# Where the scales of twelve weight blocks come from: column sums on TensorE, or squares on ScalarE and a sum over partitions on GpSimd

## The chip, the cores and the metric

One core of a Trainium2 chip runs the whole kernel. The metric is the device time of one execution in microseconds. The profile is of one such execution on the same core; its times are microseconds from the start of the span, unless they are marked ns.

Names of the engines in the profile: PE is TensorE (PEld its weight loads), DVE is VectorE, ACT is ScalarE, POOL is GpSimd, SP is the engine that issues most of the DMAs. A "q" behind a name means its sequencer, mostly DMA issues.

## The reference

Causal attention with a learned decay as bias, then a gated feed-forward network over all tokens. Sizes: 8 batches, 8 heads, 576 positions, head size 64, so 4608 tokens of width 512; hidden width 1536.

```python
scores = q @ k.T / sqrt(64);  cum = cumsum(max(s, 0))
scores = where(causal, -1e9, scores + min(-(cum_i - cum_j), 0))
attn   = softmax(scores) @ v                      # per head
x      = attn, heads side by side                 # 4608 x 512
gate   = sigmoid(x @ w_gate);  val = x @ w_val    # 512 x 1536 each
out    = (gate * val) @ w_out                     # 1536 x 512, float32
```

`q`, `k`, `v` and `s` come as float32. The three weights come as 64-bit floats, which the kernel reads as pairs of 32-bit integers.

## The kernel before, in words

**Matrix products.** Operands are split into a high and a low part in f16 and multiplied in three products (high x high, high x low, low x high). So that the parts fit f16, every operand is first multiplied by a power of two, its scale. The scale divides out again behind the product. The change is about how the scales of the weights are found.

**Weights: eighteen steps.** `wsteps` lists them. Steps 0 to 11 are for the gate and value weights, step f for the f-th block of 128 hidden columns (both matrices: 4 x 2 x 128 = 1024 numbers a partition). Steps 12 to 17 are for the output weights, two blocks of 128 hidden rows each. One step (`weight_step`) does:
- `load_weight`: DMAs of the 64-bit numbers into a room, issued from ACT's queue for steps 2 and later. Rooms are few. Before step n, `weight_step` issues loads whose room an earlier step has left.
- `decode_weight`: 64-bit floats into 32-bit ones, by one ACT copy (L298) and three DVE passes over 128x1024 (L299, L300, L301). L299 writes a first rough form `m`, whose upper 16 bits serve as a bf16 number for the column sums; L301 gives the final `a`.
- `column_bound`: eight TensorE matmuls of `ones` with that bf16 form (L310) add the columns up over all partitions into a PSUM bank. A DVE maximum over the 128 sums with its accumulator output (L313) makes one number of it. The PSUM bank is the one tag "av" (one buffer, otherwise the attention output's) in the first 40 ticks, and the tag "o" (two buffers, otherwise the output rows') after that.
- Two small DVE instructions (L332, L334) make the power of two from it.
- `split_weight`: an ACT copy with that scale gives the high part (L337), a DVE pass the low part (L338).

`column_bound` needs `m` alone, so it may run beside L300 and L301. The function `split_weight` has a second way, taken where `decode_weight` gives no `m`; before, that is for weights that come as float32, so never here. It squares `a` on ACT with a sum along each partition, adds the 128 sums over partitions on POOL (`partition_all_reduce`, result in every partition), and makes the power of two from that with `pow2_of` (two small DVE instructions).

**The order of the work.** The body is one loop over 332 ticks, five a head (one for each tile of query rows), 64 heads. The first eight heads (ticks 0 to 39) run in float32 on PE (functions named `n_...`); later ones in split f16: scores (`s_part`, L489 and L491), bias and maximum on DVE (L529), exponent on ACT (L530), high and low part of the probabilities (`p_part`: ACT L534, DVE L539 and L547), a transposing DMA, output (`av_part`, L562 to L567), `x_part` and `split_x`. Weight steps 0 to 5 are spread over ticks up to 32. From tick 44 (`NE`) on, the first two groups of 256 tokens go through the first feed-forward product, 24 units in eight ticks; each unit is 24 matmuls (L714, into the tag "gv" of two banks), a tanh on ACT (L719) and one DVE instruction (L721). Ahead of every third unit stand three weight steps and the scales of three blocks for the tanh (`inverse_weights`, `ffn_scale`); the steps of the output weights stand between the later units. After the last unit `hidden_scale` needs all scales, and only then come the output products of these two groups (`ffn_mid`: L729, L730; `ffn_out`: L744). `late_slots` then closes the pool `lp` (`ones`, the first room, small rest) and takes its place for more buffers of `x`.

The loop gives program order and priorities, not the order on the engines. `first()` raises attention of ticks 44 to 86 above the rest, so weight steps and units are work in the background there. The order on each engine is laid out when the program is built, from priority and from the time at which each instruction is expected to be ready. On the chip each engine then takes its own queue strictly in that order.

**POOL's queue** holds the all-reduces for the scales of q and k (L406) and of v (L196), the broadcasts of the decay rows (L451), masks (L511, from head 16 on), memsets (L459, L471) and the DMAs of the output rows.

The lines that the chip's time hangs on most in the units:

```python
with first(NE <= n < NOFF):
    s_part(i, NTL - 1 - t)
...
if f < NF and f % WLA == 0:
    while wnext["step"] < f + WLA:
        weight_step()
    inverse_weights(0, slice(f, f + WLA))
    ffn_scale(0, slice(f, f + WLA))
while f == 8 and wnext["step"] < NF + 1:
    weight_step()
while f >= NF and wnext["step"] < min(f + NF + WLA, len(wsteps)):
    weight_step()
emit_unit()
```

Of the kernel before, what the change touches and what calls it, by code (L numbers as in the profile page):

```python
# [10 lines left out]
F32 = mybir.dt.float32  # L11
# [7 lines left out]
P = 128  # L19
# [6 lines left out]
def tile_attention_then_gated_ffn(  # L26
# [23 lines left out]
    NTL = len(TILES)  # L50
# [4 lines left out]
    NN = H  # L55
# [7 lines left out]
    pp = ctx.enter_context(tc.tile_pool(name="pp", bufs=2, space=bass.MemoryType.PSUM))  # L63
# [160 lines left out]

    wide = w_gate.dtype == I64
    wst, wdec, wtot = {}, {}, {}

    rows_out = cp.tile([P, 2 * DM], F32, name="io")
    t2big = cp.tile([P, 2 * NF * GT], F32, name="t2f")
# [23 lines left out]
    def room(n):  # L253

        o, f = wsteps[n]
        if o == 0:
            return raw[f % 3], dec[f % 3], n - 3
        i, j, last = outroom[f // 2]
        return raw[i], dec[j], last
# [30 lines left out]
    def decode_weight(n):  # L290

        o, f = wsteps[n]
        r, a, _ = room(n)
        if not wide:
            return a.bitcast(F32), None
        m = w2all[:, f // 2].rearrange("p l h x n -> p (l h x n)") if o else w1[f].rearrange("p c g l n -> p (c g l n)")
        m = m.bitcast(I32)
        nc.scalar.activation(a.bitcast(F32), r[:, :, 1].bitcast(F32), AF.Copy, scale=2.0 ** -112)  # L298
        nc.vector.tensor_scalar(m, a, 3, 0x7FFFFFF8, ALU.logical_shift_left, ALU.bitwise_and)  # L299
        nc.vector.scalar_tensor_tensor(a, a, -0x80000000, m, ALU.bitwise_and, ALU.bitwise_or)  # L300
        nc.vector.scalar_tensor_tensor(a, r[:, :, 0], 29, a, ALU.logical_shift_right, ALU.bitwise_or)  # L301
        return a.bitcast(F32), m

    def column_bound(n, m):

        top = m.bitcast(BF16).rearrange("p (n t) -> p n t", t=2)[:, :, 1]
        early = wnext["tick"] < NTL * NN
        ps = pp.tile([P, 512], F32, tag="av" if early else "o", name=f"wps{n}", **({"bufs": 1} if early else {}))
        for c in range(8):
            nc.tensor.matmul(ps[:, :P], ones, top[:, c * P : (c + 1) * P], start=c == 0, stop=c == 7)  # L310
        tot = wp.tile([P, 1], F32, tag="wst", name=f"wtot{n}")
        junk = lp.tile([P, P], BF16, tag="wj", name=f"wj{n}")
        nc.vector.tensor_scalar(junk, ps[:, :P], 2.0 ** -100, None, ALU.max, ALU.max, accum_out=tot)  # L313
        return tot

    def split_weight(n, a, m):

        o, f = wsteps[n]
        if o:
            hi, lo = (w2all[:, f // 2, l].rearrange("p h x n -> p (h x n)") for l in range(2))  # L320
        else:
            a = a.rearrange("p (c n) -> p c n", n=P)
            hi, lo = (w1[f].rearrange("p c g l n -> p (c g) l n")[:, :, l] for l in range(2))
        if m is None:
            ss = wp.tile([P, 1], F32, tag="wss", name=f"wss{n}")
            nc.scalar.activation(hi, a, AF.Square, accum_out=ss)
            tot = wp.tile([P, 1], F32, tag="wst", name=f"wtot{n}")
            nc.gpsimd.partition_all_reduce(tot, ss, P, ADD_REDUCE)
            pow2_of(wscale[:, o, f : f + 1 + o], tot, f"w{n}")
        else:  # L330
            e = wp.tile([P, 1], I32, tag="xe", name=f"xe_w{n}")
            nc.vector.tensor_scalar(e, column_bound(n, m).bitcast(I32), 0x7F800000, None, ALU.bitwise_and)  # L332
            dst = wscale[:, o, f : f + 1 + o]
            nc.vector.tensor_scalar(dst.bitcast(I32), e.to_broadcast([P, 2]) if o else e, -1.0, 268.0 * 2.0 ** 23,  # L334
                                    ALU.mult, ALU.add)
        sc = wscale[:, o, f : f + 1]
        nc.scalar.activation(hi, a, AF.Copy, scale=sc)  # L337
        nc.vector.scalar_tensor_tensor(lo, a, sc, hi, ALU.mult, ALU.subtract)  # L338
# [21 lines left out]
        osc[b] = wp.tile([P, 1], F32, tag="osc", name=f"osc{b}", bufs=3)  # L360
        nc.vector.tensor_scalar(osc[b], gmax, sv[b][1], 2.0 ** 14, ALU.mult, ALU.mult)

    wnext = {"load": 0, "step": 0, "tick": 0}

    def weight_step():
        n = wnext["step"]
        while n and wnext["load"] < len(wsteps) and room(wnext["load"])[2] < n:
            if not NF <= wnext["load"] < NF + 2:
                load_weight(wnext["load"])
            wnext["load"] += 1  # L370
        split_weight(n, *decode_weight(n))
        wnext["step"] = n + 1
# [426 lines left out]
    for n in range(nticks + 12):  # L799
        if n == NTL * EARLY:  # L800
            more_room()
        i, t = divmod(n, NTL)
        wnext["tick"] = n
        if i < NN:
            with first():
                n_s(i, NTL - 1 - t)
# [7 lines left out]
        if 2 <= n < nticks + 2:  # L814
            a, z = divmod(n - 2, NTL)
# [5 lines left out]
        if 1 <= n < nticks + 1:  # L821
            a, z = divmod(n - 1, NTL)
# [7 lines left out]
        if 3 <= n < 3 + NTL * NN:  # L830
            with first():
                a, z = divmod(n - 3, NTL)
# [113 lines left out]
        if n >= NE and state["u"] < 2 * NF:  # L946
            fdone = min(NF, int((n - NE + 1) * FPT))
            while state["u"] < 2 * fdone:
                f = state["u"]
# [17 lines left out]
        m = n - (11 if n > 2 * NTL * H + 30 else 7)  # L967
# [42 lines left out]
```

## Time and profile before

| | |
|---|---|
| median of 3 runs | 1151.53 us (1150.67 to 1153.77) |
| the profiled execution | 1150.28 us, of it span 1148.5 us |
| PE busy | 1096.8 us (96%), 11868 matmuls |
| DVE busy | 756.4 us (66%) |
| ACT busy | 733.5 us (64%) |
| POOL busy | 199.9 us (17%) |
| mean granted clock of TensorE | 0.993 |

Busy times are shares of the whole span; the stages differ. A slice view cuts the span in 40 equal parts and gives the busy share of each in tenths. A view of windows gives busy time and, in brackets, the number of instructions for each engine in a stretch, then the granted TensorE clock. A list of waits gives who stood idle for whom, the total, how often, and the longest. A timeline gives start, length, engine, line, operation and what it writes from what; in square brackets stands the idle time ahead of it and what ended that. A chain is followed back from the last instruction to whatever released each step.

### The profile page before, as it was taken

The numbers are of one execution on the slowest core, as the hardware profiler recorded it, in microseconds if no ns is written. First come the engines' busy times: TensorE is split into PE (matmuls) and PEld (weight loads), VectorE is DVE, ScalarE is ACT, GpSimd is POOL, SyncE is SP. The second block draws the span as 40 slices with busy tenths as digits, with TensorE's granted clock in tenths as the row PEclk, the third lists the DMA queues.
The fourth block names the chain that finished last, engine by engine and source line by source line (L and its number), as shares of the span: only waits on it lengthen the run. The fifth ranks groups of instructions, "written<-read, shape, count | busy, mean of one in ns | idle before, by whom it ended". The sixth has DMA issues, their size and how long they took to land.

```text
span 1148.5 us, 30266 instructions
## 1 busy us (share of the span) xinstructions
PE 1096.8 (96%) x11868; PEld 861.6 (75%) x11868; DVE 756.4 (66%) x2212; ACT 733.5 (64%) x1437; POOL 199.9 (17%) x473
## 2 busy tenths in 40 slices
PE   6998878999999999999999999999999999999998
PEld 4776757757777887788777777778877787787775
DVE  6868989876787777665565667777777775222222
ACT  5869667867776777676665667778676765233222
POOL 3301101022232222121211122212221211000000
PEclk9999999999999999999999999999999999999999
DMA  9766986997989688866645488878787774000000
GB/s 282 218 189 140 181 178 144 174 200 154 178 159 187 150 186 158 154 139 135 148 87 130 90 175 163 170 144 175 152 159 146 142 123 88 13 20 20 1 19 19
DMA packets 445517, 157.63 MB, mean 137 GB/s; under 512 B 403583, under 2 KB 435839, under 8 KB 445374
## 3 DMA queue, kind: packets, MB, share of 16 engines
q1 hardware_dynamic: 418686, 127.38, 56.7%
q10 hardware_dynamic: 23328, 17.04, 4.9%
q0 software_dynamic: 3360, 11.27, 2.8%
q8 instruction: 93, 1.52, 0.6%
q14 instruction: 50, 0.41, 0.1%
HBM read 56.92 MB, written 9.58 MB: 58 GB/s over the span
## 4 chain that ended last, share of the span: by engine, by line
PE 72%; DMA 10%; DVE 6%; issue 5%; ACT 3%; SPq 3%; POOL 1%; ACTq 0%; DVEq 0%; POOLq 0%
PE gv L714 39%; PE o L744 21%; DMA v<-in_v_dram 3%; PE s L491 3%; PE s L489 2%; DMA T<-qk 2%; PE na_ps L662 1%; SPq L463 1%; DVE e L529 1%; PE av L564 1%; PE av L562 1%; PE av L563 1%; DMA qk<-in_q_dram 1%; DMA w2all<-in_moe_w_out_dram 1%; PE s L631 1%
## 5 line engine op out<-in xcount | busy, mean ns | idle before, releaser
L714 PE MATMUL gv<-x,w 128*128 128x256 f16 (+3 forms) x6912 | 619.2, 247 | 10.1 <-DVE t2f L721 9.1
L714 PEld LDWEIGHTS <-w 128*128 128x128 f16 x6912 | 536.0, 98 | 75.0 <-issue 11.5
L744 PE MATMUL o<-w2all,h 128*128 128x512 f16 x1296 | 313.7, 379 | 1.8 <-ACT h L729 1.8
L530 ACT ACTIVATE e<-e,em 128x576 f32<-128x576 f32 x280 | 153.2, 556 | 92.5 <-DVE em L529 89.8
L744 PEld LDWEIGHTS <-h 128*128 128x128 f16 x1296 | 123.3, 98 | 109.1 <-ACT h L729 2.1
L719 ACT ACTIVATE th<-gv,scb 128x256 f32<-128x256 f32 (+3 forms) x288 | 110.8, 410 | 138.6 <-PE gv L714 130.5
L721 DVE SCALAR_TENSOR_TENSOR t<-th,gv 128x256 f32<-128x256 f32 x192 | 80.0, 417 | 147.9 <-ACT th L719 146.8
L511 POOL TENSOR_SCALAR_AFFINE_SELECT rl<-rl 128x128 f32<-128x128 f32 (+1 forms) x240 | 85.8, 358 | 503.1 <-DVE em L529 462.3
L529 DVE CUSTOM_DVE_ANT_0 e<-s,rl,qkcf 128x576 f32<-128x576 f32 x280 | 151.5, 545 | 31.7 <-PE s L491 15.6
L729 ACT ACTIVATE h<-t,hsc 128x256 f16<-128x256 f32 x192 | 96.7, 504 | 92.4 <-DVE t L721 92.4
L539 DVE SCALAR_TENSOR_TENSOR p<-e,p 128x384 f16<-128x384 f32 x224 | 103.1, 500 | 45.1 <-ACT p L534 44.3
L730 DVE SCALAR_TENSOR_TENSOR h<-t,hsc,h 128x256 f16<-128x256 f32 x192 | 93.7, 488 | 44.9 <-ACT h L729 42.6
L534 ACT ACTIVATE p<-e 128x1152 f16<-128x1152 f32 x112 | 111.9, 1000 | 2.7
L489 PE MATMUL s<-T 128*128 128x288 f16 (+2 forms) x246 | 64.1, 278 | 7.8 <-DVE em L529 4.0
L562 PE MATMUL av<-v,pt 128*128 128x65 f16 x560 | 67.7, 193 | 2.2 <-DMA pt<-p 2.2
L451 POOL PARTITION_BROADCAST cr<-cr x63 | 59.4, 947 | 56.0 <-DMA cr<-cum_d 42.0
L563 PE MATMUL av<-v,pt 128*128 128x64 f16 x560 | 67.7, 192 | 0.0
L564 PE MATMUL av<-v,pt 128*128 128x65 f16 x560 | 67.6, 194 | 0.0
L491 PE MATMUL s<-T 128*128 128x288 f16 (+2 forms) x246 | 61.5, 277 | 4.0 <-DMA T<-T 3.9
L562 PEld LDWEIGHTS <-pt 128*128 128x128 f16 x560 | 52.5, 97 | 7.9 <-DMA pt<-p 3.1
L563 PEld LDWEIGHTS <-pt 128*128 128x128 f16 x560 | 52.5, 97 | 4.5
L564 PEld LDWEIGHTS <-pt 128*128 128x128 f16 x560 | 52.7, 97 | 0.2
(164 smaller groups left out, 1297.0 us busy)
## 6 DMA issues: line engine op xcount, KB each, us to landing
v<-v SPq DMA_DIRECT2D x56, 162.5 KB
out_dram<-io POOLq DMA_DIRECT2D x34, 256.0 KB, 3.2
v<-in_v_dram SPq DMA_DIRECT2D x64, 128.0 KB
T<-T SPq DMA_DIRECT2D x82, 72.0 KB
t2f<-in_v_dram SPq DMA_DIRECT2D x20, 288.0 KB
qk<-in_q_dram SPq DMA_DIRECT2D x17, 288.0 KB
qk<-in_k_dram SPq DMA_DIRECT2D x17, 288.0 KB
w2all<-in_moe_w_gate_dram ACTq DMA_DIRECT2D x7, 512.0 KB
```

Of the source, the lines that this page charges most:

```text
L491: nc.tensor.matmul(ps[:, : b_ - a], lhs, T[i][:, 2, a:b_], start=False, stop=not mask)
L529: nc.vector.tensor_tensor_reduce(e, ps, r, c, MASKED, ALU.add, ALU.min, acc)
L530: nc.scalar.activation(e_t[t][:, :w], e_t[t][:, :w], AF.Exp, bias=acc, scale=-1.0)
L534: nc.scalar.activation(p_s[h_][:, 0], e_s[h_], AF.Copy, scale=PSCALE)
L539: nc.vector.scalar_tensor_tensor(flat[:, LOW[t] * P : (LOW[t] + t) * P], e_t[t][:, : t * P], PSCALE, flat[:, kb * P : (kb + t) * P], ALU.m ...
L562: nc.tensor.matmul(AV[i][:, t], hi, v_[:, D : 2 * D + 1], start=kb == 0, stop=False)
L563: nc.tensor.matmul(AV[i][:, t, 0:D], hi, v_[:, 0:D], start=False, stop=False)
L564: nc.tensor.matmul(AV[i][:, t], lo, v_[:, D : 2 * D + 1], start=False, stop=False)
L714: nc.tensor.matmul(ps[:, gv, a:e], w1[f][:, cc, gv, wl], x_of(b, cc)[:, xl, c0 + a : c0 + e], start=(c == 0), stop=(c == 3 * NC - 1))
L719: nc.scalar.activation(th[:, a:e], ps[:, 0, a:e], AF.Tanh, scale=scb[b][:, f : f + 1])
L729: nc.scalar.activation(h[:, 0], t2, AF.Copy, scale=hsc[:, f : f + 1])
L744: nc.tensor.matmul(ps[:m], h[:, hl, tt * P : tt * P + m], w2[f][:, wl], start=(f == 0 and c == 0), stop=(f == NF - 1 and c == 2))
```

## The change

The first six steps keep column sums. For the other twelve `decode_weight` gives no `m` to the scale, so `split_weight` goes its second way: Square on ACT with an accumulator output, all-reduce on POOL, `pow2_of` on DVE. L299 still writes `m`, which L300 and L301 need. Column sums then occur in the first 40 ticks alone, so the choice of the PSUM tag and the count of ticks fall away.

```diff
+    NSUM = 6
...
-        return a.bitcast(F32), m
+        return a.bitcast(F32), m if n < NSUM else None
 
     def column_bound(n, m):
 
         top = m.bitcast(BF16).rearrange("p (n t) -> p n t", t=2)[:, :, 1]
-        early = wnext["tick"] < NTL * NN
-        ps = pp.tile([P, 512], F32, tag="av" if early else "o", name=f"wps{n}", **({"bufs": 1} if early else {}))
+        ps = pp.tile([P, 512], F32, tag="av", name=f"wps{n}", bufs=1)
...
-    wnext = {"load": 0, "step": 0, "tick": 0}
+    wnext = {"load": 0, "step": 0}
...
-        wnext["tick"] = n
```

The way that twelve steps now take:

```python
ss = wp.tile([P, 1], F32, tag="wss", name=f"wss{n}")
nc.scalar.activation(hi, a, AF.Square, accum_out=ss)
tot = wp.tile([P, 1], F32, tag="wst", name=f"wtot{n}")
nc.gpsimd.partition_all_reduce(tot, ss, P, ADD_REDUCE)
pow2_of(wscale[:, o, f : f + 1 + o], tot, f"w{n}")
```

## The prediction

> **What bounds the kernel now.** I read the page first, for the engines' totals and where in the span they are idle, then busy time by stretch, then the waits and the chain of work inside the one stretch that the change touches.
>
> ```profile
> span 1148.5 us, 30266 instructions
> PE 1096.8 (96%) x11868; PEld 861.6 (75%) x11868; DVE 756.4 (66%) x2212; ACT 733.5 (64%) x1437; POOL 199.9 (17%) x473
> ...
> PE   6998878999999999999999999999999999999998
> DVE  6868989876787777665565667777777775222222
> ```
>
> Forty slices of 28.7 us each. TensorE (PE) is full from slice 8 on. The first seven or eight slices, some 215 us, have holes on PE, and there VectorE (DVE) is the fuller one. A change in the weight steps can only move time in those holes. The windows say it in numbers (columns: window, length, then busy time and count per engine, granted clock, DMA share, GB/s):
>
> ```profile
> core 0: us, PE busy (x) PEld busy (x) DVE busy (x) ACT busy (x) POOL busy (x), PEclk, DMA share, GB/s
> 99.00:121.00 22.00, 17.70 (x179) 14.46 (x178) 20.40 (x64) 21.41 (x36) 1.92 (x3) 0.84 0.75 155
> 121.00:211.00 90.00, 73.27 (x820) 62.55 (x820) 83.81 (x226) 60.63 (x100) 10.28 (x14) 0.98 0.85 165
> sum 112.00, PE 90.96 PEld 77.00 DVE 104.21 ACT 82.04 POOL 12.20; mean PE 45.48 PEld 38.50 DVE 52.11 ACT 41.02 POOL 6.10
> ...
> 260.00:1148.00 888.00, 878.54 (x9910) 690.04 (x9908) 546.10 (x1616) 542.35 (x1081) 153.91 (x377) 1.00 0.60 122
> ```
>
> After 260 us PE is busy 878.5 of 888 us, and no weight step lies there. The twelve changed steps (6 to 17) have their column sums and scales between 99 and 211 us. There DVE is busy 104.2 of 112 us (93%), PE 81%, ScalarE (ACT) 73%, GpSimd (POOL) 11%. So this stretch runs on DVE's throughput, except in 99 to 121, where ACT is the fullest (21.41 of 22). What ends the idle times there:
>
> ```profile
> POOL v L471 <- PE av L564: 49.3, 3, 33.7
> ...
> PE gv L714 <- DVE t2f L721: 9.1, 6, 3.3
> ...
> ACT w2all L337 <- DVE xe_w L332: 1.4, 1, 1.4
> ...
> DVE qke L411 <- POOL qkt L406: 0.3, 1, 0.3
> ```
>
> PE's largest wait is for DVE to empty the gate/value bank (9.1 us in six waits). Only once, for 1.4 us, did a weight step's scale keep an engine waiting. POOL is nearly empty and its results are waited for 0.3 us in all, but it stands in its own queue for up to 33.7 us at a time.
>
> **The change part by part.** Steps 0 to 5 keep their column sums, in the same PSUM tag as before; the counter "tick" issues nothing. For each of the twelve other steps:
>
> *Removed from PE: eight matmuls with their weight loads. Removed from DVE: the maximum over the sums and its accumulator read.* The views of those two lines alone, for the twelve steps:
>
> ```profile
> 99.00:211.00 112.00, 7.69 (x96) 6.43 (x96) 0.95 0.83 163
> ...
> 99.00:211.00 112.00, 3.41 (x24) 0.95 0.83 163
> ```
>
> That is 7.69 us of PE busy time and 3.41 us of DVE. What an instruction keeps its engine from the next one is less, since successive ones overlap, as DVE's timeline shows:
>
> ```profile
> 122.97 0.28 DVE L313 TENSOR_SCALAR_CACHE_REDUCE wj<-wps 128x128 bf16<-128x128 f32 x1
> 123.17 0.08 DVE L313 DVE_READ_ACCUMULATOR wj<-wps 128x1 f32 x1
> 123.17 0.41 DVE L721 SCALAR_TENSOR_TENSOR t2f<-th,gv 128x256 f32<-128x256 f32 x1
> ```
>
> The next instruction starts 0.20 us after the maximum did, so DVE gets back 12 x 0.20 = 2.4 us. How much of all this stands on the chain that set the end? First and last pieces of each line in the chain between 99 and 211 us (five pieces of PE, seven of DVE):
>
> ```profile
> 99.45 0.23 PE wps L310 x4
> ...
> 106.00 0.49 PE wps L310 x8
> ...
> 108.57 0.21 DVE wj L313 x2
> ...
> 178.26 0.20 DVE wj L313 x2
> ```
>
> The five PE pieces add up to 0.96 us, the seven DVE pieces to 1.07. I take **-2.0 us**. The bounds: 0, if every freed slot becomes a wait, and -5.9 (12 x 0.49), if PE were the bound all through; the chain's own count is nearest. The two small DVE instructions that make a power of two are replaced by two of the same size: nothing.
>
> *Added to ACT: a Square over 128x1024 with an accumulator read.* Nearest rows: the same size as a plain copy (L298), and Squares with a read (L403).
>
> ```profile
> L298 ACT ACTIVATE wa<-ws x5: 1097/1131/1137, 10.6 to 190.1; 128x1024 f32<-128x1024 f32 x5
> ...
> 103.16 0.84 ACT L403 ACTIVATE jq<-qk 96x768 f16<-96x768 f32 x1 [0.19 <-DMA qk<-in_q_dram]
> 103.91 0.19 ACT L403 ACTIVATION_READ_ACCUMULATOR jq<-qk 96x1 f32 x1
> 104.00 1.13 ACT L530 ACTIVATE e<-e,em 128x320 f32<-128x320 f32 x3
> ```
>
> By the starts, a Square hands over 0.09 us before its end and the read takes 0.09, so one step keeps ACT for about 1.13 us, twelve for 13.6. ACT goes from 82.0 to 95.6 of 112 us (85%), and hidden in its 30 us of idle time, mostly. The exception is 99 to 121, with 0.6 us free and three steps (6, 7, 8) to place: up to 3 x 1.13 - 0.6 = 2.8 us would push what follows there. What follows is background work (tanh, splits), while attention carries priority, and what ends PE's waits for the bank is DVE, not ACT (9.1 us, above), so most is covered. I take **+0.5**, between 0 and +2.8 for this place. If that cover were gone, the cost would be PE's wait for the bank, row by row. The weight loads go out by ACT's own queue, behind these Squares: one Square's delay, 1.1 us, for the load below would be the most.
>
> *Moved: the scale's latency.* Before, the sums ran on PE beside DVE's last two decode passes. Now Square, all-reduce and two DVE instructions come after the last pass (L301) and before the split (L337), which is queued on ACT in order. How much room is there between those two? Step 12, then step 17:
>
> ```profile
> 147.10 1.22 DVE L301 SCALAR_TENSOR_TENSOR io<-t2f,io 128x1024 int32<-128x1024 int32 x1
> ...
> 157.41 1.15 ACT L337 ACTIVATE w2all<-io,wscale 128x1024 f16<-128x1024 f32 x1 [1.40 <-DVE xe_w L332]
> ...
> 200.94 1.21 DVE L301 SCALAR_TENSOR_TENSOR wa<-ws,wa 128x1024 int32<-128x1024 int32 x1
> ...
> 205.50 1.14 ACT L337 ACTIVATE w2all<-wa,wscale 128x1024 f16<-128x1024 f32 x1
> ```
>
> 9.1 us for step 12, 3.35 for step 17, which is the last. What has to fit: 1.13 (Square) + the all-reduce + about 0.3 for two small DVE instructions. The all-reduces of today:
>
> ```profile
> L406 POOL PARTITION_ALL_REDUCE qkt<-ssq x6: 407/408/1214, 86.3 to 241.2; - x6
> ```
>
> So 1.8 us at the median, 2.6 at the longest: hidden, **0**. It holds even for step 17. If the cover were gone it would be 1.8 to 2.6 us late on step 17, behind which the scale of the hidden layer and with it all output matmuls wait. The load on the chain that this touches is that of step 15, issued from ACT's queue right behind the split of step 12:
>
> ```profile
> 158.69 10.58 DMA w2all<-in_moe_w_out_dram
> ```
>
> It goes out later by as much as that split does.
>
> *Added to POOL: twelve all-reduces*, 12 x 0.41 = 4.9 us (at 1.21 each, 14.5) on an engine with 100 us free: nothing by itself. But two engines may get in each other's way:
>
> ```profile
> 176.33 2.52 POOL L451 PARTITION_BROADCAST cr<-cr  x2
> ...
> 176.44 1.68 DVE L301 SCALAR_TENSOR_TENSOR wa<-w2all,wa 128x1024 int32<-128x1024 int32 x1
> ```
>
> L301 takes 1.21 us alone and 1.68 beside that broadcast: 0.47 per 2.52 us of POOL work. Scaled to 4.9 us of all-reduce this is 0.9, and half of DVE's instructions would be hit: **+0.5**, between 0 and 12 x 0.47 = 5.6. [...]
>
> Sum: -2.0 + 0.5 + 0 + 0.5 = **-1.0 us** against the profiled execution's own 1150.28 us: 1149.3. The median shown, 1151.53, lies 1.25 us above that execution, so I forecast 1150.5 as a median.
>
> **The rivals.** About 0.3% (3.4 us) is what a measurement of this kernel can tell from no change.
>
> *DVE's and PE's relief counts in full (faster).* DVE is 93% busy and PE waits on it, so the 2.4 us of DVE may come out whole, and PE's freed 5.9 may fill with units that are ready. For it: the windows. Against it: the chain names those lines for 2.0 us only, and much of the rest is DMA. In the middle 4.2, so 1147.3.
>
> *ACT becomes the bound in 99 to 121 (slower).* The three Squares cost their 2.8 us there, the step 15 load goes out 1.1 late, and PE, with less to do, pauses once more long enough to lose its clock:
>
> ```profile
> 113.01 0.66 PE L686 MATMUL nx_ps<-ident,nx 128*128 128x128 f32 x2 [3.40 <-DVE x L689]
> 113.46 5.32 PE L714 MATMUL gv<-x,w 128*128 128x256 f16 x28
> ...
> 141.07 2.78 PE L714 MATMUL gv<-x,w 128*128 128x256 f16 x24
> ...
> 110.00:120.00 10.00, 6.79 (x52) 5.12 (x53) 10.00 (x28) 9.61 (x17) 0.00 (x0) 0.66 0.53 138
> ```
>
> After the 3.40 us pause 28 matmuls took 190 ns each where 116 is usual, with a granted clock of 0.66: 2.1 us. Together 2.8 + 1.1 + 2.1 - 2.0 = +4.0: 1155.5. [...] Against this rival: ACT has 29 us free right after.
>
> *An all-reduce stands behind a blocked POOL instruction (slower).* POOL takes its queue in order:
>
> ```profile
> 140.94 1.21 POOL L406 PARTITION_ALL_REDUCE qkt<-ssq  x1 [3.97 <-ACT jq L403]
> 175.86 0.12 POOL L471 MEMSET v<- 128x20 f16 x1 [33.71 <-PE av L564]
> ```
>
> A Square for step 12 would be done by 149.5. If its all-reduce is queued behind that memset it runs at 176.0, the split at about 176.7 instead of 157.4: 19 us, and ACT, in order, stands too. It decides once an all-reduce comes later than the 9.1 us of room. With half of that covered, +10 to +19; say 1166. Against it: the order is laid out by expected readiness, and so far no engine waited over 0.3 us for POOL's work.
>
> **How the numbers follow.** Hidden as summed (inside 0.3%): 0.42. Full relief: 0.26. ACT the bound: 0.19. POOL blocked: 0.13. So faster 0.26, same 0.42, slower 0.32. The forecast is the likeliest case, 1150.5, by itself 1148.1 to 1155. The range takes in nearly all of the relief (5.9 off is 1145.6, a little more for the order of instructions moving) and the ACT case, and the milder half of the POOL case: 1144 to 1160, leaving out 1 in 10 or a little more.
>
> **What would show it.** Right, if in the profile after: DVE's share of 99 to 211 stays over 90% in a stretch of the same length; ACT has some 13 us more there; twelve more all-reduces of 0.4 us with no long wait ahead of them; the last split ends within 2 us of 208; and PE from 260 on is unchanged. Wrong, if an all-reduce starts more than some 3 us after its Square, if a wait of DVE or PE for the split or tanh on ACT heads the list, or if the clock is down in more windows than now.

## The result, and the profile after

The changed kernel takes 1161.39 us (median of 8 runs, 1156.44 to 1164.92) where the kernel before takes 1151.62 (8 runs on the same chip): a ratio of 1.0076, interval 1.0052 to 1.01. The medians lie 9.8 us apart, and the new one is 1.39 us above the top of the range. The ratio, here and below, is one of means; the two means lie 8.7 us apart.

The profiled execution took 1161.32 us. Its page, busy time and slices:

```profile
span 1159.5 us, 30094 instructions
PE 1097.8 (95%) x11772; PEld 859.3 (74%) x11772; DVE 756.0 (65%) x2188; ACT 746.1 (64%) x1461; POOL 209.2 (18%) x485
...
PE   6997777799999999999999999999999999999998
...
PEclk9999899899999999999999999999999999999999
```

The span grew by 11.0 us. PE's idle time (span less busy) went from 51.7 to 61.7: +10.0. Its busy time grew by 1.0, although 96 matmuls of 7.69 us are gone; so the matmuls that are left took 8.7 us longer, and the mean granted clock fell from 0.993 to 0.984. Idle +10.0, slower matmuls +8.7, fewer matmuls -7.7 make the 11.0.

The same windows as in the prediction:

```profile
core 0: us, PE busy (x) PEld busy (x) DVE busy (x) ACT busy (x) POOL busy (x), PEclk, DMA share, GB/s
99.00:121.00 22.00, 14.79 (x113) 11.83 (x114) 21.04 (x54) 18.68 (x29) 4.17 (x6) 0.84 0.69 150
121.00:211.00 90.00, 66.65 (x727) 54.91 (x726) 80.03 (x208) 71.12 (x122) 15.66 (x22) 0.93 0.89 167
sum 112.00, PE 81.44 PEld 66.74 DVE 101.07 ACT 89.80 POOL 19.83; mean PE 40.72 PEld 33.37 DVE 50.53 ACT 44.90 POOL 9.91
...
260.00:1148.00 888.00, 880.33 (x9935) 691.21 (x9933) 547.83 (x1618) 542.67 (x1082) 153.18 (x377) 1.00 0.60 121
```

From 260 us on PE is as full as it was. In 99 to 211 it ran 840 matmuls where it ran 999 before: 96 of the missing are the sums, and 63 are other work that came later. Its clock there was lower (0.93 in the long window, 0.98 before). DVE is at 90% (93% before) and in 99 to 121 the fullest (21.04 of 22, 20.40 before); ACT is not full even there (18.68 of 22). No engine that had room is full now; the time went into PE's waits. Those between 95 and 215 us (total, times, longest), below the 9.1 us for the gate/value bank, were before:

```profile
PE s L491 <- DMA T<-T: 3.9, 4, 1.9
PE nx_ps L686 <- DVE x L689: 3.4, 1, 3.4
PE s L489 <- DMA T<-qk: 3.3, 2, 2.4
PE s L489 <- DVE em L529: 0.9, 1, 0.9
PE gv L714 <- ACT x L688: 0.4, 1, 0.4
PE av L562 <- DMA pt<-p: 0.3, 1, 0.3
```

And after:

```profile
PE av L562 <- DMA pt<-p: 14.9, 6, 5.6
PE s L489 <- DVE em L529: 4.9, 4, 2.0
PE gv L714 <- ACT x L688: 4.0, 1, 4.0
PE gv L714 <- DVE t2f L721: 3.9, 4, 1.8
...
PE nx_ps L686 <- DVE x L689: 0.7, 2, 0.5
```

The two whole lists add up to 22.0 us before and 31.7 after, +9.7, nearly all of the +10.0 of idle time. The wait for the gate/value bank (L721), the largest before with 9.1 us, fell to 3.9. In its place came attention: 14.9 us for transposed probabilities `pt`, 0.3 before in this stretch, and 4.0 for the maxima `em`, from 0.9 to 4.9. The 4.0 us in one piece for `x` on ACT stand where PE waited 3.4 us for the low part of `x` on DVE before. PE's timeline shows the waits for `x` and `pt` and what follows the longest:

```profile
113.27 0.59 PE L714 MATMUL gv<-x,w 128*128 128x256 f16 x2 [3.97 <-ACT x L688]
...
128.78 0.23 PE L562 MATMUL av<-v,pt 128*128 128x65 f16 x1 [5.56 <-DMA pt<-p]
...
129.59 6.32 PE L714 MATMUL gv<-x,w 128*128 128x256 f16 x38
```

After the 5.56 us pause 38 matmuls took 166 ns each (6.32/38) where the prediction had 116 as usual: 1.9 us on top of the pause. The granted clock was 0.67 in those 6.32 us.

What held `x` up, and where the delay of `pt` begins, stands in ACT's queue. First the timeline before:

```profile
100.41 1.14 ACT L337 ACTIVATE w<-w2all,wscale 128x1024 f16<-128x1024 f32 x1
101.45 1.15 ACT L534 ACTIVATE p<-e 128x1152 f16<-128x1152 f32 x1
...
107.63 1.14 ACT L337 ACTIVATE w<-wa,wscale 128x1024 f16<-128x1024 f32 x1
108.67 0.51 ACT L688 ACTIVATE x<-nx_ps,vsc 128x320 f16<-128x320 f32 x1
```

And after (L299 is the decode's copy, L298 before):

```profile
99.96 1.15 ACT L337 ACTIVATE w<-w2all,wscale 128x1024 f16<-128x1024 f32 x1 [0.75 <-DVE wscale L150]
101.01 1.13 ACT L337 ACTIVATE w<-wa,wscale 128x1024 f16<-128x1024 f32 x1
...
102.41 1.15 ACT L337 ACTIVATE w<-w2all,wscale 128x1024 f16<-128x1024 f32 x1
...
105.95 1.13 ACT L299 ACTIVATE w2all<-w2all 128x1024 f32<-128x1024 f32 x1
106.99 1.16 ACT L299 ACTIVATE wa<-ws 128x1024 f32<-128x1024 f32 x1
...
108.50 1.15 ACT L534 ACTIVATE p<-e 128x1152 f16<-128x1152 f32 x1
...
110.38 1.12 ACT L299 ACTIVATE w2all<-w2all 128x1024 f32<-128x1024 f32 x1
...
112.71 0.51 ACT L688 ACTIVATE x<-nx_ps,vsc 128x320 f16<-128x320 f32 x1
113.12 1.05 ACT L326 ACTIVATE w<-w2all 128x1024 f16<-128x1024 f32 x1
```

Before, the probabilities (L534) stand behind one split (L337, step 5) and start at 101.45. After, the splits of steps 6 and 7 and two copies of the decode, all of which used to come later, stand ahead of them too, and a third copy ahead of `x`. L534 starts 7.05 us later, `x` 4.04 us later. The first Square of this stretch (L326) comes only behind both. These are the same instructions in another order.

ACT is only the beginning for `pt`. Behind L534 come the low parts on DVE and the transposing DMA, and there the chain that set the end runs now:

```profile
112.81 6.01 DMA pt<-p
118.90 0.73 ACT p L534
...
120.50 8.24 DMA pt<-p
129.78 6.13 PE gv L714 x38
```

The transposing DMA that PE then waits for went out at 109.79 us before, 10.5 us ahead of its use at 120.34, and goes out at 120.50 after. Between 90 and 235 us these DMAs are 22.8% of the chain; before, none of them is among its longest pieces. Weight loads, 512 KB each, are issued just ahead of both DMAs (111.51 and 111.92 us, then 119.07 and 119.67); before, such a pair goes out only behind both, at 115.05 and 115.50. That the loads are what makes them 6 and 8 us long is my guess from these times; no run shows it.

The order of every queue is laid out anew when the program is built. Of the entries that both finished programs have, at least 1052 of 22852 in PE's queue (matmuls and weight loads) stand in another order than before, 254 of 2170 in DVE's and 128 of 1383 in ACT's. In both profiled executions the instructions then ran in the order of their queue, as far as the names of what they write tell it: ACT's 1348 before and 1360 after, DVE's elementwise passes (1326 and 1314), and GpSimd's masks and memsets (330 each).

### The profile page after: what moved, and what is told of

It reads as the page before. It is cut to its first block, busy times and chain, and to the rows that moved or that the text cites. A ratio compares the mean times of both kernels' runs of the same rounds, so it can differ in the third digit from the quotient of the medians.

```text
span 1159.5 us, 30094 instructions
## 1 busy us (share of the span) xinstructions
PE 1097.8 (95%) x11772; PEld 859.3 (74%) x11772; DVE 756.0 (65%) x2188; ACT 746.1 (64%) x1461; POOL 209.2 (18%) x485
## 4 chain that ended last, share of the span: by engine, by line
PE 77%; DMA 10%; DVE 4%; ACT 4%; issue 2%; SPq 2%; POOL 0%; ACTq 0%; DVEq 0%; POOLq 0%
PE gv L714 41%; PE o L744 22%; DMA v<-in_v_dram 3%; DMA pt<-p 3%; PE s L489 3%; PE s L491 3%; PE av L562 1%; PE av L564 1%; PE av L563 1%; DMA qk<-in_q_dram 1%; DMA T<-qk 1%; PE s L631 1%; PE na_ps L662 1%; DVE e L529 1%; SPq L463 1%
## 5 line engine op out<-in xcount | busy, mean ns | idle before, releaser
L721 DVE SCALAR_TENSOR_TENSOR t<-th,gv 128x256 f32<-128x256 f32 x192 | 80.1, 417 | 146.6 <-ACT th L719 146.5
L534 ACT ACTIVATE p<-e 128x1152 f16<-128x1152 f32 x112 | 112.0, 1000 | 6.6 <-DMA pt<-p 4.3
L562 PE MATMUL av<-v,pt 128*128 128x65 f16 x560 | 67.9, 193 | 15.1 <-DMA pt<-p 14.9
L489 PE MATMUL s<-T 128*128 128x288 f16 (+2 forms) x246 | 64.5, 281 | 12.3 <-DVE em L529 9.4
L491 PE MATMUL s<-T 128*128 128x288 f16 (+2 forms) x246 | 63.5, 283 | 2.0 <-DMA T<-T 2.0
```

What stands on the lines that cost most here:

```text
L489: nc.tensor.matmul(ps[:, : b_ - a], lhs, T[i][:, 0, a:b_], start=True, stop=False)
L491: nc.tensor.matmul(ps[:, : b_ - a], lhs, T[i][:, 2, a:b_], start=False, stop=not mask)
L534: nc.scalar.activation(p_s[h_][:, 0], e_s[h_], AF.Copy, scale=PSCALE)
L562: nc.tensor.matmul(AV[i][:, t], hi, v_[:, D : 2 * D + 1], start=kb == 0, stop=False)
```

## The experiments

Four theories came first. LOAD: the Squares on ACT, 13.6 us by the prediction and 12.6 by the page (746.1 less 733.5), cost the time. PATH: the scale's detour over ACT and GpSimd makes what waits for it late. CLOCK: PE, without its sums, pauses longer, and its granted clock is lower behind the pauses, as in the row above (0.67 behind 5.56 us). LAYOUT: any added instruction changes the queues, whatever it does; in the last six runs it is called ORDER. Each ratio is to the kernel before, run on the same chip, with its 95% interval in brackets.

### Part of the change, and its load alone

Squares for steps 6 to 11 only, and for 12 to 17 only:

```diff
-        return a.bitcast(F32), m
+        return a.bitcast(F32), None if 6 <= n < NF else m    # e1_sq_hidden
+        return a.bitcast(F32), m if n < NF else None         # e2_sq_out
```

> Squares for steps 6 to 11 (gate and value weights) only; the six steps of the output weights keep column sums. Theory PATH (the scale's way is longer and goes through ACT's queue twice and POOL's once, so the last splits and with them the scale of the hidden layer come late): those last splits are of output weights, so this kernel stays near the one before, 1151 to 1155 us, and the last split ends near 208 us. Theory LOAD (13.6 us more on ACT, worst in 95 to 130 us where ACT has no room): steps 6 to 11 do that harm, so most of the 10 us comes, 1158 to 1161. Theory LAYOUT (any edit that moves the order of instructions costs or gives several us): anything, with no relation to e2.

> The opposite half: squares for steps 12 to 17 (output weights) only, column sums for the first twelve. PATH: most of the 10 us comes, 1157 to 1161, and the last split ends near 219 us. LOAD: 95 to 130 us is as before, so 1151 to 1154. If both halves' differences add up to about 10 us, the cost is spread; if they do not add up, the order of instructions has a share.

Measured: 1.004 (1.0022 to 1.0058) and 1.0034 (1.0015 to 1.0052). That is 4.6 and 3.9 us, together about the 8.7 us of the whole change. Neither PATH (nearly all in the second) nor LOAD (nearly all in the first) had this, and no single step seemed to be to blame.

The kernel before with twelve Squares that nobody uses, and with 24:

```diff
+        if n >= 6:
+            for r_ in range(2):                              # e3_idle_sq: once
+                idle = wp.tile([P, 1], F32, tag="wss", name=f"wss{n}_{r_}")
+                nc.scalar.activation(hi, a, AF.Square, accum_out=idle)
```

> The kernel before with the twelve Squares added on ACT (128x1024 with an accumulator read), their result unused; the scale still comes by column sums. ACT's load is that of the change, the scale's path that of before, though the split stands behind the Square on ACT. LOAD: 1158 to 1162, PE's granted clock down in 110 to 160 us as after. PATH: within 3 us of before, 1150 to 1155.

> The idle Squares of e3_idle_sq twice in every one of the twelve steps, so 27 us more on ACT instead of 13.6 (both results unused). LOAD: about twice the 5 us of e3_idle_sq or more, 1160 to 1167, since ACT would be full from 99 to 211 us. LAYOUT: the same 4 to 5 us, 1154 to 1158.

Measured: 1.0043 (1.0024 to 1.0062) and 1.0145 (1.0126 to 1.0164). The first median, 1156.79 us, lies between what PATH and LOAD had, the second, 1168.17, a little above LOAD's range.

The same twelve idle Squares over one column of each partition, and the changed kernel with Squares over 128 of the 1024 columns (its scale is taken from those alone; the lines shown are those of the output weights):

```diff
+            nc.scalar.activation(hi[:, 0:1], a[:, 0:1], AF.Square, accum_out=idle)   # n1_one_column
-            nc.scalar.activation(hi, a, AF.Square, accum_out=ss)
+            nc.scalar.activation(hi[:, 0:P], a[:, 0:P], AF.Square, accum_out=ss)     # e4_small_sq
```

> The idle Squares of the kernel e3_idle_sq cut to one column each (the scale by column sums, the Squares' result unused): the same instructions in the same places of the program, about 0.3 us of ACT each in place of 1.13, next to no load. LOAD: the 5 us of e3_idle_sq shrink to at most 1.5, so 1150 to 1153. LAYOUT (any edit of these steps leads to another order of instructions and costs some 4 us): 1154 to 1157.

> The changed kernel with each Square over 128 of the 1024 columns, so the scale is taken from an eighth of the numbers. ACT is relieved of some 9 us of the 13.6; path, waits and POOL stay. LOAD: most of the loss is gone, 1151 to 1155. PATH: a Square's own 0.75 us less in each of three rounds of rooms is all that is won, so 1157 to 1160.

Measured: 0.9995 (0.9977 to 1.0013) and 1.0041 (1.002 to 1.0062).

This looked like a clean curve: idle Squares of one column cost nothing, twelve whole ones 5 us, 24 whole ones 16.7 us. I took LAYOUT as refuted by the 0.9995, LOAD as shown for 5 us, and the rest as open between PATH and CLOCK. The reading was wrong. Each of these kernels has its own queues; in PE's queue of the one-column kernel at least 971 of 23044 entries stand in another order than before, about as many as in the changed kernel.

### The sums kept, the scale first, the detour alone

```diff
+        if n >= NSUM:
+            sums_only(n, m)                  # e5_sums_kept: the eight matmuls, result unused
+            with first():                    # p1_prompt: Square, all-reduce and pow2_of
```

> The changed kernel with the column sums' matmuls of the twelve steps kept on TensorE, their sums unused. PE has 7.7 us more to do and fewer empty stretches. Theory CLOCK (the removed matmuls had filled pauses of PE, and longer pauses lower its clock): the granted clock returns to some 0.99 and the time falls, 1154 to 1159. LOAD and PATH: no gain, up to 5 us more, 1160 to 1167.

> The changed kernel with Square, all-reduce and the two small DVE instructions of each of the twelve steps raised to the priority of the attention, so that they are queued as soon as they are ready; work and path are the same. PATH by queueing (scale ready late because each link stands behind other work in its queue): the last split is some 5 to 8 us earlier and 3 to 6 us come back, 1155 to 1159. LOAD: no gain, since the Squares now stand ahead of exponents, 1160 to 1165.

Measured: 1.0053 (1.0033 to 1.0072) and 1.0101 (1.0078 to 1.0125). The median of the first, 1157.38 us, is where CLOCK had it (1154 to 1159). But its interval overlaps that of the changed kernel, and its order is its own. The second says nothing on PATH: raising the priority moved three small DVE instructions and left all else in the changed kernel's order. It is nearly a second measurement of that kernel, and shows how far two sets of runs of one order can lie apart, 0.0025.

The detour without Squares (sums, then a hop over GpSimd), and the detour with small Squares for steps 12 to 17:

```diff
+            if n >= 6:                       # q1_pool_hop, on the kernel before
+                hop = wp.tile([P, 1], F32, tag="wss", name=f"hop{n}")
+                nc.gpsimd.partition_all_reduce(hop, top, P, ADD_REDUCE)
+                top = hop
```

> The kernel before, with one link put into the scale's chain for steps 6 to 17: the bound from the column sums goes through an all-reduce on GpSimd before DVE makes the power of two (a sum of 128 equal values, the exponent's constant raised by 7). ACT gets nothing, PE keeps its sums. LOAD (ACT's Squares cost the time, all of it): no change, within 2 us of before. PATH (the detour of the scale over GpSimd's queue and back costs the 4 us that small Squares still cost): 3 to 5 us slower. CLOCK (the sums that PE no longer does leave it idle and its clock lower): no change, since PE keeps them.

> The kernel before, with the change made for steps 12 to 17 alone and with Squares over 128 of 1024 columns (the scale is taken from those columns only). The whole Squares cost 3.9 us there (ratio 1.0034). LOAD: next to nothing left, within 1.5 us of before. PATH or CLOCK: about 2 us left, half of the 4.1 us that small Squares in all twelve steps cost; were the detour of the last step's scale the whole of it, all 4 us.

Measured: 0.9972 (0.9954 to 0.999) and 1.0059 (1.004 to 1.0078). No theory had these. The kernel with the hop, which adds work to the path of twelve scales, was faster. Small Squares in six steps cost 6.8 us where whole ones had cost 3.9. The intervals of the two overlap, but LOAD had next to nothing left here.

### ACT relieved

The decode's copy on GpSimd for steps 6 to 17, in the kernel before and in the changed one:

```diff
+        if n >= 6:
+            nc.gpsimd.tensor_scalar(a.bitcast(F32), r[:, :, 1].bitcast(F32), 2.0 ** -112, None, ALU.mult)
+        else:
             nc.scalar.activation(a.bitcast(F32), r[:, :, 1].bitcast(F32), AF.Copy, scale=2.0 ** -112)
```

> The kernel before, with the plain copy that starts the decode of steps 6 to 17 (1.13 us on ACT) moved to GpSimd. ACT's load in the weight steps goes down by as much as the Squares raised it. LOAD, if it is linear: some 5 us faster, 1146. LOAD, if before it was ACT's last free share that counted: no change. Rival PORT: a 128x1024 float copy on GpSimd holds up DVE beside it, 0.47 us for each 2.5 us as the row of the prediction had it: with 2 to 3 us a copy that is 12 x 0.5 = 6 us slower, and the decode chain of each step is 1 to 2 us longer.

> The changed kernel with that same copy on GpSimd for steps 6 to 17, so that ACT's load in the weight steps is again that of the kernel before. LOAD: the 5 us of the Squares come back and 4 to 5 us stay, ratio near 1.004. Rival PORT: GpSimd's copies hold up DVE and stand ahead of the all-reduces: no better than the changed kernel's 1.0076, up to 1.012.

Measured: 1.0628 (1.0605 to 1.0651) and 1.0599 (1.0573 to 1.0624), some 70 us slower. The PORT rival had the sign, and neither the size nor the cause. One of these copies on GpSimd, in the first kernel:

```profile
102.71 2.84 POOL L299 TENSOR_SCALAR w2all<-w2all 128x1024 f32<-128x1024 f32 x1 [6.89 <-issue]
```

It takes 2.84 us, with 6.89 us ahead of it in which GpSimd waits for nothing that the profile shows. DVE's passes wait for it (12.3 and 16.0 us at the longest). So these two kernels say nothing on LOAD.

### The same queues with and without the load

To tell order from load, the order has to stand still. In the next kernels the queues are laid out as in an earlier kernel, and only then is each Square narrowed or widened, by replacing its access patterns in the finished program. Order, waits and buffers stay entry by entry. (The kernels labelled m are cut ones, w4 is widened.)

```diff
+    for blk in nc.main_func.blocks:               # behind the layout
+        new = list(blk.instructions)
+        for k, ins in enumerate(new):
...
+                for d in ap[1:-1]:                # Squares over 1024 columns: input and output
+                    d[1] = 1
+                ap[-1][1] = 1                     # 128 in ma and mb; the reverse in w4
+                side[0] = _copy.replace(side[0], ap=ap)
+            new[k] = _copy.replace(ins, ins=sides[0], outs=sides[1])
```

> The kernel before with 24 idle Squares (1.0145, 16.7 us), every queue in exactly that kernel's order, but each Square cut to one column after the order was laid out. The work on the chip is that of before within 24 x 0.3 us of ACT. LOAD: all of the 16.7 us gone, 0.998 to 1.002. ORDER (the queues laid out anew, not the work, cost the time): still 1.010 to 1.015. Half and half: 1.007.

> The changed kernel, every queue in exactly its order, each Square cut to 128 of its 1024 columns afterwards (the scale is then taken from those columns only). LOAD: the 5 us that the dose gave come back, ratio 1.003 to 1.005, as in the kernel laid out with small Squares (1.0041). ORDER: no change from the changed kernel, 1.0076 to 1.010.

> The kernel with small Squares (1.0041), every queue in exactly its order, each Square widened to all 1024 columns afterwards, so that it does just the work of the changed kernel in another order. LOAD: 5 us more than with small Squares, 1.008 to 1.010. ORDER: as with small Squares, 1.004. That the Squares now take longer than the layout counted on may cost beyond that.

> The changed kernel with the column sums kept and unused (1.0053), every queue in exactly its order, each Square cut to 128 columns afterwards: detour of the scale, but neither load nor missing sums. LOAD alone: within 0.2% of before. PATH (the detour): 1.003 to 1.005. CLOCK (the missing sums): within 0.2% of before.

> The kernel before with 12 idle Squares (1.0043), every queue in exactly that kernel's order, each Square cut to one column afterwards. LOAD: 0.998 to 1.002. ORDER: 1.0043 still.

That the load was in fact cut, by the Squares' rows in the groups of the kernel with 24 whole ones, then of the same queues cut:

```profile
L339 ACT ACTIVATE w<-w2all x8: 1054/1060/1064, 112.3 to 159.7; 128x1024 f16<-128x1024 f32 x8
```

```profile
L339 ACT ACTIVATE w<-w2all x8: 188/192/206, 110.4 to 159.2; 128x1 f16<-128x1 f32 x8
```

All ratios to the kernel before:

| queues of | whole Squares | Squares cut | whole less cut |
|---|---|---|---|
| the changed kernel | 1.0076 (1.0052 to 1.01) | 1.008 (1.0059 to 1.01) | -0.0004 |
| small Squares | 1.0032 (1.0018 to 1.0045) | 1.0041 (1.002 to 1.0062) | -0.0009 |
| 12 idle Squares | 1.0043 (1.0024 to 1.0062) | 1.007 (1.0043 to 1.0097) | -0.0027 |
| 24 idle Squares | 1.0145 (1.0126 to 1.0164) | 1.0123 (1.0107 to 1.014) | +0.0022 |
| sums kept | 1.0053 (1.0033 to 1.0072) | 1.0036 (1.0022 to 1.005) | +0.0017 |

Along a row the order is the same and the load differs by 12 x 0.75 us or more. The mean of the last column is 0.0000. With intervals of about 0.002 to either side, a difference is known to 0.0028 and the mean of five to 0.0013, that is 1.5 us. By the scatter of the five themselves the mean is known to 0.0025 only, that is 3 us. LOAD had 5 us for twelve Squares and 16.7 for 24; it has fallen. The 9 to 21 us of work on ACT cost 0 within 3 us.

Down a column the orders differ, and in two places the work is the same. The changed kernel's work took 1.0076 in its own order (1.0101 in the second measurement) and 1.0032 in the order laid out for small Squares: 5 us (2 to 8 by the two intervals) between the two. The kernel before with twelve idle one-column Squares took 0.9995 in one order and 1.007 in another: 8.6 us (5 to 12). Nothing differs but the order, with the waits and buffers that come with it. ORDER is shown: for the changed kernel's work it is worth 5 us between these two orders, of the 8.7 that were to be explained. What makes the 3.7 us that are left in the better order is not shown.

The trace shows it in place too. The changed kernel with its Squares cut to 128 columns: PE's waits in 95 to 215 us, the Square's row, and ACT's timeline:

```profile
PE av L562 <- DMA pt<-p: 13.7, 5, 6.4
PE s L489 <- DVE em L529: 5.7, 5, 2.0
PE gv L714 <- ACT x L688: 4.2, 1, 4.2
```

```profile
L326 ACT ACTIVATE w<-w2all x4: 293/298/309, 88.2 to 148.9; 128x128 f16<-128x128 f32 x4
```

```profile
104.19 1.12 ACT L299 ACTIVATE w2all<-w2all 128x1024 f32<-128x1024 f32 x1
105.22 1.15 ACT L299 ACTIVATE wa<-ws 128x1024 f32<-128x1024 f32 x1
...
106.72 1.15 ACT L534 ACTIVATE p<-e 128x1152 f16<-128x1152 f32 x1
...
108.61 1.12 ACT L299 ACTIVATE w2all<-w2all 128x1024 f32<-128x1024 f32 x1
...
110.94 0.50 ACT L688 ACTIVATE x<-nx_ps,vsc 128x320 f16<-128x320 f32 x1
```

With Squares of 0.30 us the same three waits are there, in the same sizes: 13.7 us for `pt`, 5.7 for the maxima, 4.2 for `x`, behind the same copies. The two transposing DMAs go out at 110.83 and 118.53 us here, and behind the second PE waits 6.39 us for `pt`, its longest. In the other order, with whole Squares (its line numbers are three higher), PE's waits and the Square's row:

```profile
PE av L565 <- DMA pt<-p: 6.8, 5, 2.1
...
PE gv L717 <- ACT x L691: 2.1, 1, 2.1
```

```profile
L329 ACT ACTIVATE w<-w2all x4: 1040/1053/1061, 87.7 to 149.3; 128x1024 f16<-128x1024 f32 x4
```

These two waits are half as long, with the full load. Other waits took a part of their place: PE's nine largest in this stretch add up to 28.6 us here, 30.2 with the Squares cut and 31.5 in the changed kernel.

### The faster order again

The kernel with the hop over GpSimd, unchanged, a second time:

> The same kernel again as the one with the hop over GpSimd (0.9972, interval 0.9954 to 0.999). If its order is a better one by 3 us: 0.9954 to 0.999 again. If that was chance: 0.999 to 1.001.

Measured: 0.9976 (0.9958 to 0.9994), 1147.67 us where the kernel before took 1150.66. Twice it beats the kernel before by some 3 us. Its order is the likely reason: it does all that the kernel before does and twelve all-reduces more (L335 of that kernel).

```profile
L335 POOL PARTITION_ALL_REDUCE hop<-wtot x12: 385/450/3867, 107.9 to 199.2; - x12
```

That it is the order and not the hop is only argued; the hop was not taken out of that order.

### What stays open

Whether the detour or the missing sums cost something beside the order. The ten kernels that make a scale by Squares (r2 left aside) lie at 1.0032 to 1.0101, in six orders. The seven that make it from the sums (r1 left aside) lie at 0.9972 to 1.0145, in four. The groups overlap, so neither cost is shown or excluded; but all six orders of the first group are slower than the kernel before, by 3.7 us at least. The kernel with the sums kept and the load cut, 1.0036, is where PATH alone put it and not where LOAD or CLOCK did, but its order is its own as well. Nor was it found why an order with Squares is laid out as it is.

## Why the prediction was wrong

- **Removed from PE and DVE, -2.0: not seen.** The wait that this relief was to shorten did shrink, from 9.1 to 3.9 us, but other waits took its place. The chain of before, off which the price was read, was gone with the order.
- **Added to ACT, +0.5: not contradicted.** The five pairs give 0 within 3 us for all of the Squares. ACT's idle time, the cover named, had the room: its busy time grew by 12.6 us, and by 7.8 in 99 to 211 us, not the 13 that were to be seen there. Two Squares ran before that stretch.
- **Latency of the scale, 0: the room was read off an order that was gone.** The last split (L338) ended at 220.7 us and not within 2 us of 208. But in the one-column kernel too the last split is late: the Square that stands ahead of it on ACT starts at 208.6 us, where the split's own ACT copy (L337) started at 205.50 before. That kernel's ratio is 0.9995; lateness of this size alone is not the cost.
- **GpSimd beside DVE, +0.5, and the rival of a blocked POOL: no cost of either.** Twelve all-reduces took 0.45 us at the median, by their group and by one row of GpSimd's timeline:

```profile
L328 POOL PARTITION_ALL_REDUCE wtot<-wss x12: 383/452/1017, 98.3 to 211.5; - x12
```

```profile
121.55 0.46 POOL L328 PARTITION_ALL_REDUCE wtot<-wss  x1 [6.75 <-ACT w L326]
```

  From step 8 on each came within 1 us of its Square's read; GpSimd mostly stood ready and waited for ACT (eight times, 20.9 us in all), as in the second row. For steps 6 and 7 it ran 33 and 11 us later, which the prediction had named as a sign of being wrong; but their splits came earlier than before (101.01 and 102.41 us, 107.63 and 116.03 before). DVE beside an all-reduce shows no cost either: in the kernel with the hop, passes of L300 and L301 beside all-reduces of up to 3.87 us took 1.21 to 1.22 us, where 1.21 to 1.23 is the median before. The row of 1.68 us that gave the +0.5 was beside a broadcast. So was a pass of 1.74 us after, at 131.15 us (its L301, L300 before), but another L301, wholly beside a broadcast in the kernel before at 193.92 us, took 1.21. That half of DVE's instructions would be hit, as the +0.5 takes it, no run shows.
- **The rival that ACT becomes the bound in 99 to 121 us** (1155.5 us) came nearest in place: a PE pause of 3.97 us for `x` on ACT, and behind it a granted clock of 0.50 (115 to 119 us). Its cause was wrong: ACT has 3.3 us free there, and the pause is as long with Squares of 0.30 us.

**The step that failed** stands in one clause of the range, "a little more for the order of instructions moving". Every edit was costed against the queues of before, though the planner lays all of them out anew for any edit. So the waits and the cover of the sum were read off queues that were gone, and the term for the order itself was put at next to nothing without a reason. That term had to be as wide as the draw of an order: the runs show 5 and 8.6 us between two orders of the same work, and 0.997 to 1.0145, that is -3 to +17 us, over all the orders, whose work is not quite the same. Beside it every other term of the sum is small. With an own chance for a worse draw the range would have reached past 1161. What the other 3.7 of the 8.7 us are stays open.

Of what was to show it, "PE from 260 on unchanged" held, and "DVE over 90%" barely (101.07 of 112). The sign named for being wrong, that the clock is down in more windows, came true: 0.93 in 121 to 211 after 0.98.

## What to carry to other kernels

Where a planner lays out the queues, an edit is two changes: its own, and a new order of everything around it. Before a few tenths of a per cent are put down to the edit, run the edit's order with its load taken out, and the same work in a second order. One neutral addition that costs nothing doesn't rule the order out (0.9995 here, but 1.007 for the same twelve one-column Squares in another order, and 1.0123 for 24 of them), and a dose that rises smoothly doesn't show a load, if each dose has its own order.

## What the runs showed of the hardware that was not expected

- 9 to 21 us more on ACT, in the stretch where the prediction had it at 73% busy, cost nothing measurable (0 within 3 us) while the order stood still.
- An elementwise copy on GpSimd between its all-reduces and broadcasts cost not 2.84 us but 9.7 us, with 6.89 us of idle issue ahead of it; with twelve such copies the kernel took 70 us more. Such idle issue stands ahead of four of the twelve copies (29.3 us in all; 7.09 us ahead of the one at 133.08) and ahead of the all-reduce behind the first (6.05 us at 111.86).
